# Softmax of a fused attention and MLP kernel: the scale moves into q on GpSimd, the row's small sums move between engines

## The chip, the cores and the metric

The kernel runs on one core of a Trainium2 chip. The core has five instruction queues that matter here, each worked off in order: TensorE (PE, with its weight loads PEld), VectorE (DVE), ScalarE (ACT), GpSimd (POOL) and SyncE (SP), from which all the DMAs are issued. The time is the device time of one execution in microseconds (us). The profile is that of one execution.

## What is computed

Eight batches of eight heads of attention over 576 positions with head width 64, and an MLP on the joined heads. Cut to what matters:

```python
scale = 1.0 / np.sqrt(q.shape[-1])                      # 1/8
scores = scale * np.matmul(q, k.transpose(0, 1, 3, 2))
thresh = np.max(scores, axis=-1, keepdims=True) - tau   # tau = 0.02
scores = np.where(scores >= thresh, scores, -1e9)
scores = scores - np.max(scores, axis=-1, keepdims=True)
attn = np.exp(scores)
attn = attn / (np.sum(attn, axis=-1, keepdims=True) + 1e-09)
out = np.matmul(attn, v)
# then, on out as (4608, 512):
h = x @ w_in                                            # 512 -> 2048
g = h * np.tanh(np.log1p(np.exp(np.minimum(h, 20.0))))  # for h <= 20
return g @ w_out                                        # 2048 -> 512
```

If tau is negative no score reaches its threshold; then all of a row's scores are -1e9, and the reference's row is uniform, 1/576.

## The kernel before, in words

Two heads make a pair; there are 32 pairs, and each has nine tiles of 128 rows of scores (2 x 576 rows), so the attention is a loop over 288 tiles, here numbered from 0. One tile goes through these steps, spread over several turns of the loop `for g in range(NT + 5)` (L665):

- PE multiplies 128 rows of q with 576 columns of k into the PSUM tile `s` (`scores`; two buffers).
- DVE takes the negated row maximum into column 0 of a small tile `st` (`row_max`), makes the scaled maximum (column 2) and the threshold (column 1, L405 and L406), and ACT makes `e = exp(scale * s + bias)` (L407).
- DVE multiplies `e` with the mask `s >= threshold` into `p` and sums the row into column 3 (`masked`, L412).
- In the next turn the sum's two small followers are made: column 5, 1/576 where the sum is 0 (`un`), and column 4, the sum plus 1e-9 (`de`), in `total` on DVE. From tile 54 on (`UNV`) column 5 is made by POOL in `masked` instead. Then `normalise`: DVE's RECIPROCAL makes column 6 from column 4, and POOL makes `p = p * reciprocal + un`.
- Two turns on, PE transposes `p`, ACT and DVE take it out of PSUM (`hi`, `lo`, `tk`), PE multiplies it with v (`y`), ACT copies y (`x`, `yo`) and POOL adds the two (`x<-x,yo`).

In the first four pairs (tiles 0 to 35) some operands are plain fp32: half of q (`a in plain`) and of k and all of v come by DMA straight into their tiles, and the rest, as all of q, k and v from tile 36 on, is split into a rounded part and a remainder. For q: the DMA brings a raw tile `r`, ACT casts all 128 rows to `q`, and POOL overwrites the lower 64 rows with the remainder `r - q` (L340 and L341). q is split in four pieces a pair, k in four, v in two. The raw tiles have four buffers.

Nothing here is put in order by a scheduler: `InOrder` (L82) chains each engine's instructions in the order in which the Python code makes them, so every engine's queue is the loop body as written. Only the DMAs on SP are moved by the framework. In a turn g, POOL's queue holds: `normalise` of tile g-1, the y adds, the splits of q, k, v and x that fall due ("chores"), parts of the w_in decoding (up to tile 53 or so), and, from tile 54 on, `un` of tile g. DVE's holds: maximum of g, `total` of g-1, threshold of g, RECIPROCAL of g-1, `lo` and `tk`, mask of g.

From tile 42 on, PE also runs the first MLP product, a number of matmuls a turn that a table (`MIX`) sets, so that it fills each turn; its results leave by ACT (`hst`). The table has 18 entries: the loop repeats itself every two pairs. After the attention come the last MLP pieces and the second product, which the change doesn't touch.

All of these instructions are issued by one helper line, so the profile shows L92 for each of them (L91 in the changed kernel): they are told apart by engine, operation and tile names. `st` is the small tile, `p<-p,st` on POOL is `normalise`, `p<-s,st,e` on DVE the mask.

Of the kernel before, what the change touches and what calls it, by code (L numbers as in the profile page):

```python
# [5 lines left out]
F32 = mybir.dt.float32  # L6
F32R = mybir.dt.float32r
U32 = mybir.dt.uint32
AF = mybir.ActivationFunctionType
ALU = mybir.AluOpType  # L10
# [4 lines left out]
P = 128  # L15
B, H, S, D = 8, 8, 576, 64
# [12 lines left out]
UNV = 54  # L29
# [6 lines left out]
HB = S // 2  # L36
# [36 lines left out]
SCALE = 1.0 / float(D) ** 0.5  # L73
# [4 lines left out]
def fv(ap):  # L78
    return ap.bitcast(F32)
# [78 lines left out]
def attention_moe(tc, q, k, v, tau, w_in, w_out, out):  # L158
    nc = tc.nc
    from contextlib import ExitStack  # L160

    with ExitStack() as outer:
# [8 lines left out]
        back = cst.tile([P, 1], F32, name="back")  # L171
# [95 lines left out]
        nc = Engines(tc)  # L267
        with ExitStack() as first:
# [6 lines left out]
            with ExitStack() as att:  # L275
# [36 lines left out]
                def prep(pi):  # L312
# [12 lines left out]
                    def part(src, n):  # L325
                        r = raw.tile([P, 320], F32, name="r")
                        nc.sync.dma_start(r[:, :n], src)
                        return r[:, :n]

                    def q_part(c):  # L330
                        a, half = divmod(c, 2)
                        sl = slice(half * 320, (half + 1) * 320)
                        at = slice(c * 320, (c + 1) * 320)
                        if a in plain:
                            nc.sync.dma_start(qs[a][:D, sl], q[pi, :D, at])
                            return skip
                        r = part(q[pi, :, at], 320)

                        def split():
                            nc.scalar.copy(qs[a][:, sl], r)  # L340
                            nc.gpsimd.tensor_tensor(qs[a][D:, sl], r[D:], fv(qs[a][D:, sl]), ALU.subtract)  # L341

                        return split
# [59 lines left out]
                def exponential(s, st, e):  # L403
                    nm = st[:, 0:1]
                    nc.vector.tensor_scalar(st[:, 2:3], nm, SCALE, None, ALU.mult)  # L405
                    nc.vector.tensor_scalar(st[:, 1:2], nm, -1.0, back, ALU.mult, ALU.subtract)  # L406
                    nc.scalar.activation(e, s[:, :, :HB], AF.Exp, bias=st[:, 2:3], scale=SCALE)  # L407

                def masked(g, s, st, e, p):
                    p = p.rearrange("p (a b) -> p a b", a=2)  # L410
                    th, su, un = (st[:, i:i + 1] for i in (1, 3, 5))
                    nc.vector.scalar_tensor_tensor(p, s[:, :, :HB], th, e, ALU.is_ge, ALU.mult, accum_out=su)  # L412
                    if g >= UNV:
                        nc.gpsimd.tensor_scalar(un, su, 0.0, 1.0 / S, ALU.is_le, ALU.mult)
                    return p

                def total(g, st):
                    if g < UNV:
                        nc.vector.tensor_scalar(st[:, 5:6], st[:, 3:4], 0.0, 1.0 / S, ALU.is_le, ALU.mult)
                    nc.vector.tensor_scalar(st[:, 4:5], st[:, 3:4], 1e-9, None, ALU.add)  # L420

                def normalise(st, p):
                    de, un, rc = (st[:, i:i + 1] for i in range(4, 7))
                    nc.vector.reciprocal(rc, de)
                    nc.gpsimd.tensor_scalar(p, p, rc, un, ALU.mult, ALU.add)
# [182 lines left out]
                NT = NPAIRS * 9  # L608
# [48 lines left out]
                pairs[0]["ops"], todo = prep(0)  # L657
                splits = [todo[i]() for i in FIRST[:3]]
                nc.sync.dma_start(back, tau)
# [3 lines left out]
                nc.vector.tensor_scalar(back, back, 1.0 / SCALE, None, ALU.mult)  # L663
                begin(0)
                for g in range(NT + 5):  # L665
# [28 lines left out]
                    if 1 <= g <= NT:  # L694
                        total(g - 1, tiles[g - 1]["st"])
# [255 lines left out]
```

## Time and profile before

| | |
|---|---|
| median of 3 runs | 1341.53 us (1339.64 to 1341.58) |
| the profiled execution | 1341.68 us, its span 1339.9 us |
| PE, DVE, ACT, POOL busy over the span | 98%, 84%, 74%, 65% |
| TensorE clock granted, mean | 0.995 |
| tiles 0 to 35 | first 117 us |
| tiles 36 to 53 | next 67 us |
| tiles 54 to 286 | 184 to 900.5 us |
| second product and the rest | last 439 us |

How to read it: the span is the time from the first to the last instruction on the core. The share of an engine that is busy is a mean over stages with different limits; a view by windows shows them apart. PE's matmuls overlap each other, and the ends of them are modelled, so that a PE that is shown busy need not be at its peak. In lists by time a row is: start, length, engine, line, operation, output and inputs, and in brackets how long the engine stood idle before it and what ended that. Instructions of one engine can overlap by some 0.05 to 0.1 us, so a row's length is a little more than the step to the next start.

### The profile page before, as it was taken

How to read it: one execution, taken by the hardware profiler on the slowest of the kernel's cores; microseconds unless marked ns; L12 is line 12 of the kernel's file. 1: busy time of each engine (PE TensorE's matmuls, PEld its weight loads, DVE VectorE, ACT ScalarE, POOL GpSimd, SP SyncE). 2: the span in 40 equal slices, each digit the busy share in tenths (PEclk: the TensorE clock that was granted, in tenths of full speed). 3: DMA queues.
4: the chain of work that ended last, by engine and by line, in shares of the span. 5: the costliest groups of instructions: out<-in, count | busy, mean ns of one | idle time of the engine just before them, and what ended most of it. 6: DMA issues, size and time to landing. Idle time of an engine off the chain costs nothing.

```text
span 1339.9 us, 29650 instructions
## 1 busy us (share of the span) xinstructions
PE 1317.0 (98%) x9799; PEld 1244.9 (93%) x9799; DVE 1123.4 (84%) x3018; ACT 989.0 (74%) x2052; POOL 872.7 (65%) x1191
## 2 busy tenths in 40 slices
PE   9998899999999999999999999999999999999998
PEld 7555889999999999999999999999979999999998
DVE  6999999999999999999999999995986666676664
ACT  5888788888888888888888888875665556555552
POOL 5778888788787887878878788763403333434431
PEclk9999999999999999999999999999999999999999
DMA  5333454333343333433334333314744443444440
GB/s 155 92 98 107 119 170 128 91 101 109 90 123 95 105 103 91 118 95 113 101 91 115 97 109 107 95 44 132 234 142 148 129 142 120 133 134 142 142 127 32
DMA packets 151913, 154.77 MB, mean 116 GB/s; under 512 B 35536, under 2 KB 128720, under 8 KB 151760
## 3 DMA queue, kind: packets, MB, share of 16 engines
q1 hardware_dynamic: 151760, 152.87, 38.3%
q8 instruction: 78, 1.28, 0.4%
q14 instruction: 75, 0.61, 0.1%
HBM read 105.64 MB, written 47.19 MB: 114 GB/s over the span
## 4 chain that ended last, share of the span: by engine, by line
PE 90%; DVE 5%; ACT 3%; issue 1%; DMA 1%; POOL 0%; DVEq 0%; ACTq 0%; POOLq 0%; SPq 0%
PE o L92 27%; PE h L92 27%; PE s L92 14%; PE y L92 12%; PE tp L92 9%; DVE st L92 1%; PE t L92 1%; DVE p L92 1%; DVE dec L92 1%; DVE w2l L92 1%; ACT e L92 1%; PE warm L92 1%; ACT w L92 0%; ACT dec L92 0%; DMA hd<-hst 0%
## 5 line engine op out<-in xcount | busy, mean ns | idle before, releaser
L92 PE MATMUL h<-xh,w1h 128*128 128x288 f32 x1024 | 302.3, 295 | 1.0 <-ACT hst L92 1.0
L92 PE MATMUL h<-xl,w1h 128*128 128x288 f32 x1024 | 302.4, 295 | 0.0
L92 PE MATMUL h<-xh,w1l 128*128 128x288 f32 x1024 | 302.2, 295 | 0.0
L92 POOL TENSOR_SCALAR p<-p,st 128x576 f32<-128x576 f32 x288 | 244.9, 850 | 57.7 <-DVE st L92 35.0
L92 POOL TENSOR_TENSOR z<-z 128x256 f32<-128x256 f32 x128 | 124.4, 976 | 223.0 <-DVE z L92 214.2
L92 PE MATMUL s<-k,q 128*128 128x288 f32 (+1 forms) x1280 | 253.5, 323 | 8.5 <-DVE p L92 8.2
L92 DVE SCALAR_TENSOR_TENSOR p<-s,st,e 128x576 f32<-128x576 f32 x288 | 235.1, 816 | 20.4 <-ACT e L92 10.4
L92 ACT ACTIVATE e<-s,st 128x576 f32<-128x576 f32 x288 | 214.4, 744 | 36.4 <-DVE st L92 31.7
L92 DVE TENSOR_TENSOR gl<-z,gh 128x1792 fp32r<-128x1792 f32 (+1 forms) x72 | 141.7, 1969 | 108.2 <-ACT gh L92 108.2
L92 ACT CAST gh<-z 128x1792 fp32r<-128x1792 f32 (+1 forms) x72 | 116.5, 1620 | 150.2 <-issue 81.2
L92 DVE TENSOR_REDUCE st<-s 128x1 f32<-128x576 f32 x288 | 216.7, 752 | 3.0 <-PE s L92 2.9
L92 PEld LDWEIGHTS s<-k,q 128*128 128x128 f32 (+1 forms) x1280 | 181.6, 189 | 38.3 <-DVE p L92 23.9
L92 DVE TENSOR_TENSOR lo<-tp,hi 128x512 fp32r<-128x512 f32 (+1 forms) x280 | 174.8, 633 | 49.6 <-ACT hi L92 42.7
L92 PEld LDWEIGHTS h<-xh,w1h 128*128 128x128 f32 x1024 | 192.5, 188 | 1.5 <-ACT hst L92 1.4
L92 PEld LDWEIGHTS h<-xh,w1l 128*128 128x128 f32 x1024 | 192.5, 188 | 0.0
L92 PEld LDWEIGHTS h<-xl,w1h 128*128 128x128 f32 x1024 | 192.4, 188 | 0.0
L92 PE MATMUL tp<-ident,p 128*128 128x128 f32 x1152 | 174.4, 274 | 3.6 <-DVE lo L92 2.4
L92 ACT CAST hi<-tp 128x512 fp32r<-128x512 f32 (+1 forms) x280 | 149.9, 546 | 35.8 <-PE tp L92 32.9
L92 PEld LDWEIGHTS tp<-ident,p 128*128 128x128 f32 x1152 | 138.9, 140 | 13.6 <-issue 5.7
L92 POOL TENSOR_TENSOR x<-x,yo 64x256 f32<-64x256 f32 (+1 forms) x112 | 89.9, 803 | 88.2 <-ACT yo L92 85.1
L92 PE MATMUL o<-gh,sl 128*128 128x256 f32 x512 | 144.5, 282 | 0.0
L92 PE MATMUL o<-gl,sh 128*128 128x256 f32 x512 | 143.8, 281 | 0.0
(76 smaller groups left out, 3249.8 us busy)
## 6 DMA issues: line engine op xcount, KB each, us to landing
z<-hd SPq DMA_DIRECT2D x144, 256.0 KB, 3.1
r<-q SPq DMA_DIRECT2D x120, 160.0 KB, 2.3
r<-k SPq DMA_DIRECT2D x120, 160.0 KB, 2.2
out_t<-c SPq DMA_DIRECT2D x36, 256.0 KB, 2.5
r<-v SPq DMA_DIRECT2D x56, 160.0 KB, 2.3
dec<-w_in SPq DMA_DIRECT2D x32, 256.0 KB, 3.1
hd<-hst SPq DMA_DIRECT2D x16, 512.0 KB, 3.3
w<-w_out SPq DMA_DIRECT2D x16, 512.0 KB, 4.5
```

The lines of the kernel that those rows point to most:

```text
L92: made = method(*args, **kwargs)
```

## The change

- q's pieces are multiplied by `slope` (the scale, 1/8, or 0 where tau is negative) on POOL, in place in the raw tile, before ACT casts them. The two plain pieces of each of the first four pairs, which came by DMA straight into place, now come into a raw tile too and go through POOL.
- `s` is then scaled already, so ACT's exponent takes the negated maximum (column 0) itself as its bias. The DVE instruction that scaled it (column 2) is gone from all 288 tiles.
- `un` is gone. With slope 0 all scores are 0; with the threshold raised to 3e38 below the maximum (`far`), all pass, and the row is uniform.
- `de`, the sum plus 1e-9, moves from DVE to POOL for all tiles, into `masked`. RECIPROCAL stays on DVE.
- tau is loaded first; three small DVE instructions make `slope`, `far` and `back` ahead of the first split.

```diff
-UNV = 54
...
-        back = cst.tile([P, 1], F32, name="back")
+        back, slope, far = (cst.tile([P, 1], F32, name=n) for n in ("back", "slope", "far"))
...
-                    def part(src, n):
+                    def part(src, n, rows=slice(0, P)):
                         r = raw.tile([P, 320], F32, name="r")
-                        nc.sync.dma_start(r[:, :n], src)
-                        return r[:, :n]
+                        nc.sync.dma_start(r[rows, :n], src)
+                        return r[rows, :n]
...
-                        if a in plain:
-                            nc.sync.dma_start(qs[a][:D, sl], q[pi, :D, at])
-                            return skip
-                        r = part(q[pi, :, at], 320)
+                        rows = slice(0, D) if a in plain else slice(0, P)
+                        r = part(q[pi, rows, at], 320, rows)
 
                         def split():
-                            nc.scalar.copy(qs[a][:, sl], r)
-                            nc.gpsimd.tensor_tensor(qs[a][D:, sl], r[D:], fv(qs[a][D:, sl]), ALU.subtract)
+                            if a in plain:
+                                nc.gpsimd.tensor_scalar(qs[a][:D, sl], r, slope[:D], 0.0, ALU.mult, ALU.add)
+                            else:
+                                nc.gpsimd.tensor_scalar(r, r, slope, 0.0, ALU.mult, ALU.add)
+                                nc.scalar.copy(qs[a][:, sl], r)
+                                nc.gpsimd.tensor_tensor(qs[a][D:, sl], r[D:], fv(qs[a][D:, sl]), ALU.subtract)
...
                     nm = st[:, 0:1]
-                    nc.vector.tensor_scalar(st[:, 2:3], nm, SCALE, None, ALU.mult)
                     nc.vector.tensor_scalar(st[:, 1:2], nm, -1.0, back, ALU.mult, ALU.subtract)
-                    nc.scalar.activation(e, s[:, :, :HB], AF.Exp, bias=st[:, 2:3], scale=SCALE)
+                    nc.scalar.activation(e, s[:, :, :HB], AF.Exp, bias=nm)
 
                 def masked(g, s, st, e, p):
                     p = p.rearrange("p (a b) -> p a b", a=2)
-                    th, su, un = (st[:, i:i + 1] for i in (1, 3, 5))
+                    th, su, de = (st[:, i:i + 1] for i in (1, 3, 4))
                     nc.vector.scalar_tensor_tensor(p, s[:, :, :HB], th, e, ALU.is_ge, ALU.mult, accum_out=su)
-                    if g >= UNV:
-                        nc.gpsimd.tensor_scalar(un, su, 0.0, 1.0 / S, ALU.is_le, ALU.mult)
+                    nc.gpsimd.tensor_scalar(de, su, 1e-9, None, ALU.add)
                     return p
 
-                def total(g, st):
-                    if g < UNV:
-                        nc.vector.tensor_scalar(st[:, 5:6], st[:, 3:4], 0.0, 1.0 / S, ALU.is_le, ALU.mult)
-                    nc.vector.tensor_scalar(st[:, 4:5], st[:, 3:4], 1e-9, None, ALU.add)
-
                 def normalise(st, p):
-                    de, un, rc = (st[:, i:i + 1] for i in range(4, 7))
-                    nc.vector.reciprocal(rc, de)
-                    nc.gpsimd.tensor_scalar(p, p, rc, un, ALU.mult, ALU.add)
+                    rc = st[:, 5:6]
+                    nc.vector.reciprocal(rc, st[:, 4:5])
+                    nc.gpsimd.tensor_scalar(p, p, rc, 0.0, ALU.mult, ALU.add)
...
                 pairs[0]["ops"], todo = prep(0)
+                nc.sync.dma_start(back, tau)
+                nc.vector.tensor_scalar(slope, back, 0.0, SCALE, ALU.is_ge, ALU.mult)
+                nc.vector.tensor_scalar(far, back, 0.0, 3e38, ALU.is_lt, ALU.mult)
+                nc.vector.tensor_tensor(back, back, far, ALU.add)
                 splits = [todo[i]() for i in FIRST[:3]]
-                nc.sync.dma_start(back, tau)
...
-                nc.vector.tensor_scalar(back, back, 1.0 / SCALE, None, ALU.mult)
...
-                    if 1 <= g <= NT:
-                        total(g - 1, tiles[g - 1]["st"])
```

How the queues move, at tiles 91 to 93, in the stretch where the loop has become regular. What a row waits for stands in brackets; of a semaphore's name the part ahead of the underscore is the engine that raises it, or a DMA's.

POOL before, from `un` of tile 91 to `normalise` of tile 92 (`st<-st` is `un`, `p<-p,st` is `normalise`, `q_4470<-r` a piece of q):

```order
L92 TENSOR_SCALAR st<-st 128x1 [waits DVE_49]
L92 TENSOR_SCALAR p<-p,st 128x576 [waits DVE_49,Pool_49]
L92 TENSOR_TENSOR x<-x,yo 64x320 [waits Activation_49,Pool_49]
L92 TENSOR_TENSOR q_4470<-r,q_4470 64x320 [waits DMAHW3_49,Activation_49]
L92 TENSOR_SCALAR st<-st 128x1 [waits DVE_49,Pool_49]
L92 TENSOR_SCALAR p<-p,st 128x576 [waits DVE_49,PE_49,Pool_49]
```

and after, the same stretch (`st<-st` is now `de`, `r<-r,slope` the scaling of q's piece):

```order
L91 TENSOR_SCALAR st<-st 128x1 [waits DVE_49]
L91 TENSOR_SCALAR p<-p,st 128x576 [waits DVE_49]
L91 TENSOR_TENSOR x<-x,yo 64x320 [waits Activation_49,Pool_49]
L91 TENSOR_SCALAR r<-r,slope 128x320 [waits DMAHW3_49,Pool_49]
L91 TENSOR_TENSOR q_4349<-r,q_4349 64x320 [waits Activation_49]
L91 TENSOR_SCALAR st<-st 128x1 [waits DVE_49,Pool_49]
L91 TENSOR_SCALAR p<-p,st 128x576 [waits DVE_49,PE_49]
```

The small instruction stays at its place in POOL's queue, behind the tile's adds and splits, but makes another number; one instruction is added ahead of the remainder of q.

DVE before, from RECIPROCAL of tile 91 to that of tile 92 (`st<-st 128x1 x2` are `de` of the tile before and the scaled maximum, `st<-st,back` is the threshold):

```order
L92 RECIPROCAL st<-st 128x1 [waits DVE_49]
L92 TENSOR_TENSOR lo<-tp,hi 128x4x128 [waits Activation_49]
L92 TENSOR_TENSOR tk<-t_4751,tk 64x128 [waits PE_49,Activation_49]
L92 TENSOR_TENSOR tk<-t_4751,tk 64x128
L92 SCALAR_TENSOR_TENSOR p,st<-s,st,e 128x576 [waits DVE_49,Activation_49]
L92 TENSOR_REDUCE st<-s 128x1 [waits PE_49,Pool_49]
L92 TENSOR_SCALAR st<-st 128x1 [waits DVE_49] x2
L92 TENSOR_SCALAR st<-st,back 128x1
L92 RECIPROCAL st<-st 128x1 [waits DVE_49]
```

and after:

```order
L91 RECIPROCAL st<-st 128x1 [waits Pool_49]
L91 TENSOR_TENSOR lo<-tp,hi 128x4x128 [waits Activation_49]
L91 TENSOR_TENSOR tk<-t_4623,tk 64x128 [waits PE_49,Activation_49]
L91 TENSOR_TENSOR tk<-t_4623,tk 64x128
L91 SCALAR_TENSOR_TENSOR p,st<-s,st,e 128x576 [waits DVE_49,Activation_49]
L91 TENSOR_REDUCE st<-s 128x1 [waits PE_49]
L91 TENSOR_SCALAR st<-st,back 128x1 [waits DVE_49]
L91 RECIPROCAL st<-st 128x1 [waits Pool_49]
```

Two small instructions are gone here (three in tiles 0 to 53), and RECIPROCAL waits for POOL, where it waited for DVE itself.

ACT before, at the next piece of q (`x<-y` and `yo<-y` are the copies of y):

```order
L92 COPY x<-y 64x256 [waits PE_49]
L92 COPY yo<-y 64x256 [waits Pool_49]
L92 CAST q_4470<-r 128x320 [waits DMAHW4_49]
L92 CAST k_4468<-r 128x320 [waits DMAHW5_49]
L92 CAST hi<-tp 128x4x128 [waits PE_49]
L92 ACTIVATE e<-s,st 128x576 [waits DVE_49,Activation_49]
```

and after:

```order
L91 COPY x<-y 64x256 [waits PE_49]
L91 COPY yo<-y 64x256 [waits Activation_49]
L91 CAST q_4349<-r 128x320 [waits Pool_49]
L91 CAST k_4347<-r 128x320 [waits DMAHW5_49]
L91 CAST hi<-tp 128x4x128 [waits PE_49]
L91 ACTIVATE e<-s,st 128x576 [waits DVE_49,Activation_49]
```

The order is the same; the cast of q waits for POOL's scaling instead of a DMA.

## The prediction

> **What bounds the kernel now.** I read the page's totals, then the windows by stage, then the groups of POOL and DVE, then the list by time at one tile. The page's first part:
>
> ```profile
> PE 1317.0 (98%) x9799; PEld 1244.9 (93%) x9799; DVE 1123.4 (84%) x3018; ACT 989.0 (74%) x2052; POOL 872.7 (65%) x1191
> ```
>
> PE is nearly always busy, which hides where the slack lies. By stage (columns: PE, PEld, DVE, ACT, POOL busy, clock, DMA):
>
> ```profile
> 0.00:117.00 117.00, 113.51 (x562) 69.92 (x563) 98.72 (x361) 87.11 (x220) 83.83 (x104) 1.00 0.40 118
> 117.00:184.00 67.00, 57.16 (x366) 48.40 (x365) 64.64 (x211) 54.39 (x140) 57.50 (x70) 0.95 0.45 133
> 184.00:900.50 716.50, 716.41 (x5501) 706.95 (x5500) 660.29 (x2152) 610.42 (x1468) 577.74 (x874) 1.00 0.36 102
> ```
>
> and the mask's instructions on DVE in the same windows (two rows a tile, so 36, 18 and 233 tiles):
>
> ```profile
> 0.00:117.00 117.00, 29.50 (x72) 1.00 0.40 118
> 117.00:184.00 67.00, 14.73 (x36) 0.95 0.45 133
> 184.00:900.50 716.50, 192.26 (x466) 1.00 0.36 102
> ```
>
> So from 184 us on a tile takes 716.5 / 233 = 3.075 us, 55.35 us for the 18 tiles after which the loop repeats; PE has no idle time there, DVE is busy 92%, POOL 81%. The first maximum stands at 7.33:
>
> ```profile
> 7.33 0.76 DVE L92 TENSOR_REDUCE st<-s 128x1 f32<-128x576 f32 x1 [2.75 <-PE s L92]
> ```
>
> The first 36 tiles thus take (117 - 7.3) / 36 = 3.05 us each, the next 18 take 3.72; there DVE (84% and 96%) is closest to the limit. What the change saves on DVE can shorten only these 54 tiles. What it does to POOL concerns all 288.
>
> **DVE, what is removed.** The list by time, DVE at tiles 91 and 92:
>
> ```profile
> 301.34 0.15 DVE L92 RECIPROCAL st<-st 128x1 f32<-128x1 f32 x1
> 302.23 0.59 DVE L92 TENSOR_TENSOR tk<-t,tk 64x128 fp32r<-64x128 f32 x2
> 302.86 0.82 DVE L92 SCALAR_TENSOR_TENSOR p<-s,st,e 128x576 f32<-128x576 f32 x1
> 303.60 0.75 DVE L92 TENSOR_REDUCE st<-s 128x1 f32<-128x576 f32 x1
> 304.27 0.27 DVE L92 TENSOR_SCALAR st<-st 128x1 f32<-128x1 f32 x2
> 304.58 0.15 DVE L92 RECIPROCAL st<-st 128x1 f32<-128x1 f32 x1
> 306.15 0.75 DVE L92 TENSOR_REDUCE st<-s 128x1 f32<-128x576 f32 x1
> ```
>
> Its group, 630 rows over the kernel, says 147 ns each (and no idle time ahead of RECIPROCAL, the last column):
>
> ```profile
> L92 DVE TENSOR_SCALAR st<-st 128x1 f32<-128x1 f32 x630 | 78.2, 147 | 0.1
> L92 DVE RECIPROCAL st<-st 128x1 f32<-128x1 f32 x288 | 44.1, 153 | 0.0
> ```
>
> and ACT's exponent of tile 93 in the list by time:
>
> ```profile
> 304.63 0.74 ACT L92 ACTIVATE e<-s,st 128x576 f32<-128x576 f32 x1
> ```
>
> The small rows overlap: the pair at 304.27 is 0.27 long in all and runs partly in the tail of the maximum (303.60 + 0.75 = 304.35). ACT's exponent starts at 304.63, 0.09 behind the pair's end. Started by the maximum itself it could start at 304.44, 0.19 earlier. A tile without `tk`, 2.55 us from maximum to maximum here, could then take DVE 2.4; one with `tk` (0.59 more, part of it covered) some 2.9. If that were all, the first 54 tiles would gain at most 54 x 0.19 = 10 us, and the stage that PE fills nothing.
>
> **POOL, what is added.** The groups, all tiles together:
>
> ```profile
> L92 POOL TENSOR_SCALAR p<-p,st 128x576 f32<-128x576 f32 x288 | 244.9, 850 | 57.7 <-DVE st L92 35.0 <-DVE dec L92 2.6 <-DMA dec<-w_in 1.6
> L92 POOL TENSOR_TENSOR k<-r,k 128x320 fp32r<-128x320 f32 x120 | 104.8, 880 | 9.8 <-ACT k L92 5.9 <-DMA r<-q 0.7
> L92 POOL TENSOR_TENSOR q<-r,q 64x320 fp32r<-64x320 f32 x120 | 104.6, 881 | 11.4 <-DMA r<-k 2.3 <-DVE p L92 1.7 <-DVE dec L92 1.3
> L92 POOL TENSOR_TENSOR xl<-x,xh 128x288 fp32r<-128x288 f32 x64 | 51.9, 812 | 12.3 <-ACT xh L92 12.3
> L92 POOL TENSOR_SCALAR st<-st 128x1 f32<-128x1 f32 x234 | 51.4, 220 | 8.4 <-DVE p L92 2.5
> L92 POOL TENSOR_TENSOR vs<-r,vs 128x320 fp32r<-128x320 f32 x56 | 49.1, 877 | 1.2 <-ACT vs L92 0.7
> L92 POOL TENSOR_TENSOR x<-x,yo 64x320 f32<-64x320 f32 x56 | 49.0, 875 | 65.4 <-ACT yo L92 64.1 <-DVE st L92 1.2
> L92 POOL TENSOR_TENSOR x<-x,yo 64x256 f32<-64x256 f32 x56 | 40.9, 731 | 22.8 <-ACT yo L92 21.0
> ```
>
> `de` costs POOL 0.22; from tile 54 on it replaces `un` at the same price. The scaling of a q piece is a TENSOR_SCALAR of 128x320. No row shows one; the nearest is `normalise` (850 ns for 576 elements) with the 128x1 row as its fixed part: 0.22 + 0.63 x 320/576 = 0.57. I take 0.55; the bounds are 0.47 (850 x 320/576) and 0.88 (the two-operand rows of 320). The Trainium skill (GPSIMD Engine Reference, 3.1 Elementwise and 4.1 Engine selection) has one-input work on GpSimd at about line rate, 1.03 cycles an element, but sends elementwise work to VectorE; at the 1.2 GHz of its example 320 elements would take an estimated 0.27 us and the sum below would be 27 us smaller. `normalise` at 850/576 = 1.48 ns an element disagrees, and I go by it.
>
> **The new wait, where I see the cost.** RECIPROCAL now waits for POOL's `de`, and behind it in DVE's queue stand `lo`, `tk` and the next mask. POOL at the same tiles:
>
> ```profile
> 301.26 0.22 POOL L92 TENSOR_SCALAR st<-st 128x1 f32<-128x1 f32 x1
> 301.67 0.83 POOL L92 TENSOR_SCALAR p<-p,st 128x576 f32<-128x576 f32 x1 [0.19 <-DVE st L92]
> 303.86 0.88 POOL L92 TENSOR_TENSOR x<-x,yo 64x320 f32<-64x320 f32 x1 [1.36 <-ACT yo L92]
> 304.70 0.89 POOL L92 TENSOR_TENSOR q<-r,q 64x320 fp32r<-64x320 f32 x1
> 305.68 0.22 POOL L92 TENSOR_SCALAR st<-st 128x1 f32<-128x1 f32 x1
> ```
>
> The row at 305.68 is the place where `de` of tile 92 will stand. The mask ended at 303.68, RECIPROCAL ran at 304.58: POOL comes there 2.0 us after the mask and 1.1 us after RECIPROCAL. Today nobody but POOL needs that row. After the change DVE stands still until it is done, and POOL in turn stands still until RECIPROCAL answers, since only `normalise` follows. From one RECIPROCAL to the next a tile then takes the longer of two loops: DVE's 2.4 or 2.9, and POOL's. The answers between engines, by rows:
>
> ```profile
> 941.43 2.45 POOL L92 TENSOR_TENSOR s<-s,w 128x1024 uint32<-128x1024 uint32 x1 [2.67 <-DVE s L92]
> 943.92 1.05 ACT L92 CAST w2h<-s 128x1024 fp32r<-128x1024 f32 x1 [1.69 <-POOL s L92]
> 13.42 0.15 DVE L92 RECIPROCAL st<-st 128x1 f32<-128x1 f32 x1
> 13.68 0.83 POOL L92 TENSOR_SCALAR p<-p,st 128x576 f32<-128x576 f32 x1 [1.64 <-DVE st L92]
> 2.96 0.46 ACT L92 CAST q<-r 128x320 fp32r<-128x320 f32 x1 [0.94 <-DMA r<-q]
> 3.56 0.86 POOL L92 TENSOR_TENSOR q<-r,q 64x320 fp32r<-64x320 f32 x1 [2.26 <-DMA r<-k]
> ```
>
> From POOL to ACT 0.04 (taken for POOL to DVE too; the other bound is the 0.19 above), from DVE to POOL 0.11, from ACT to POOL 0.14. POOL's loop without any split: `de` 0.22 + 0.04 + RECIPROCAL 0.15 + 0.11 + `normalise` 0.81 = 1.33 (of each POOL row I count 0.04 less than its length, for the overlap with the next). A piece of q grows from 0.84 to scaling 0.55 + 0.04 + cast 0.46 + 0.14 + 0.84 = 2.03, since scaling and remainder are neighbours in POOL's queue and the cast lies between them.
>
> For 18 tiles: 18 x 1.33 + 8 q x 2.03 + 8 k x 0.84 + 4 v x 0.84 + 4 x 0.83 and 4 x 0.69 for y + 4 xl x 0.77 = 59.4 us, already over 55.35. The loops are uneven: by the order in the queue they are, in us, 6.2, 1.3, 4.2, 1.3, 4.9, 2.9, 2.9, 3.8, 2.2, 4.2, 5.4, 3.0, 5.0, 2.0, 2.9, 2.0, 2.9, 2.2. Seven lie under DVE's loop, and filling them up adds 3.9: 63.3. Then the y adds wait for ACT, as they do now:
>
> ```profile
> POOL x L92 <- ACT yo L92: 85.1, 70, 7.7
> ```
>
> 85.1 us over 112 adds is 0.76 each; I charge it to the four adds that stand in a long loop behind a short one, where POOL is not late already: 3.0, in all 66.4 a cycle, 11.0 more than now.
>
> **The sum**, against the profiled execution's 1341.7 us (span 1339.9 and 1.8 around it; 0.15 above the median of the runs): 12 cycles from tile 54 to 269 give 12 x 11.0 = 132. The last 18 tiles have no loads left: +2. Tiles 0 to 35, with two split and two plain q pieces a pair and the w_in work on POOL, come by the same rule to 3.33 instead of 3.05 a tile, +10; tiles 36 to 53 to 4.3 instead of 3.7, +9. At the start tau is issued first, ahead of q,
>
> ```profile
> 2.12 0.43 SPq L659 DMA_DIRECT2D back<-tau  x1
> ```
>
> and the first scaling stands ahead of the first scores, 0.43 + 0.55: +1. The three small DVE instructions there run while DVE has nothing to do. Together +154: **1496 us**. Costed at nothing: ACT's cast waits for POOL with `hi`, the next exponent and `hst` behind it; it is covered because DVE waits too. Without that cover PE falls late, and the short loops cannot be shorter than PE's present tiles (3.24 and 2.55 above), some 19 us more. The eight plain q transfers now hold raw buffers; a raw buffer is freed later by what the loop is longer, and SP's queue with it, which I leave uncosted.
>
> **Bounds.** Scaling at 0.47 or 0.88: -8 or +32. The reply from POOL at 0.19 instead of 0.04: +21. No y waits: -36.
>
> **The rivals.** (A) The above: 1496. (B) Long and short loops even out, since ring buffers let DVE and POOL drift: then only POOL's total counts, 59.4 a cycle, +49 and some +8 before tile 54: 1399. For it: `s` and `p` have two buffers each. Against: RECIPROCAL and `de` tie the two engines in every tile, and no buffer lies between them. (C) PE, now with idle time in each long loop, gets a lower clock. The second window shows it, 0.95 over 67 us with PE busy 57 of 67, which is 6.7 us at half speed, 3.35 us of work lost. If each of the five longest loops of a cycle brought one such spell, 16.8 us of PE work would be lost against 11.0 of slack, 5.8 a cycle, 70 in all: 1566. For it: loops of 5 to 6 us with 3 us of PE work. Against: the first window kept 1.00. The Trainium skill (TensorE: Matmul & The Clock Gate, Part 1) has the clock halved after an idle window of about 3.4 us, which the uneven loops come close to. (D) Not slower: POOL is late in the trace only because nobody hurries it. If `de` ends within 0.9 us of the mask's end (303.68 to 304.58), RECIPROCAL waits for nothing, the 0.19 a tile is won in the first 54 tiles, and the time is 1331. It decides where POOL has no y add or split between `normalise` and `de`; in 16 of 18 tiles it has one. (E) The waits are real, but PE's work hides them and the gain pays for the rest: within 0.2%, about what a measurement of this kernel can tell from no change (its runs spread 0.15%): 1342.
>
> **How the numbers follow.** A 0.65, B 0.14, C 0.16, D 0.03, E 0.02. Slower 0.95, same 0.02, faster 0.03. The range takes in A with its bounds (1452 to 1549), goes down part of the way to B and up past C: 1430 to 1580; what it leaves out is most of B, D and E, under 2 in 10.
>
> **What would show it.** In the changed profile: DVE's idle time ahead of RECIPROCAL, ended by POOL's `st`, of the order of 100 us or more, where it was 0.0; the tiles of the regular stretch at some 3.7 us instead of 3.075 and uneven; PE idle there. POOL's scaling near 0.55 us with ACT's cast between it and the remainder. If RECIPROCAL hardly waits, the whole account is wrong; if it waits and tiles are near 3.3, B was right; a clock under 0.97 in the regular stretch means C.

## The result: 1616.7 us, slower by a fifth

The changed kernel takes 1616.66 us (median of 4 runs, 1611.8 to 1622.13), the kernel before 1341.36 beside it: a ratio of 1.206 (95% interval 1.202 to 1.210). The forecast, 1496 us with a range of 1430 to 1580, had the direction and named both new waits, one of them at no cost; it was 121 us short. The profiled execution of the changed kernel ran 1615.56 us, its span 1613.8, its mean granted clock 0.95.

The totals of the page, and the waits of the changed kernel (columns: who waited for whom, us in total, times, longest):

```profile
PE 1418.9 (88%) x9799; PEld 1309.7 (81%) x9799; DVE 1079.7 (67%) x2390; ACT 991.5 (61%) x2052; POOL 929.2 (58%) x1373
```

```profile
DVE st L91 <- POOL st L91: 350.8, 192, 4.9
...
ACT q L91 <- POOL r L91: 170.5, 120, 2.7
POOL x L91 <- ACT yo L91: 130.6, 98, 7.6
PEld tp L91 <- POOL st L91: 124.2, 66, 3.5
...
PE tp L91 <- DVE lo L91: 110.1, 64, 3.3
```

No engine is full any more; everyone waits for someone. The groups of instructions of the changed kernel (behind the bar: busy time, mean ns of one; then the idle time ahead of them and what ended it):

```profile
L91 DVE RECIPROCAL st<-st 128x1 f32<-128x1 f32 x288 | 46.3, 161 | 352.0 <-POOL st L91 350.8
L91 POOL TENSOR_SCALAR r<-r,slope 128x320 f32<-128x320 f32 x120 | 65.0, 541 | 8.1 <-DMA r<-q 2.7
L91 ACT CAST q<-r 128x320 fp32r<-128x320 f32 x120 | 55.1, 459 | 170.5 <-POOL r L91 170.5
L91 POOL TENSOR_TENSOR x<-x,yo 64x320 f32<-64x320 f32 x56 | 48.3, 862 | 93.3 <-ACT yo L91 93.3
L91 PE MATMUL tp<-ident,p 128*128 128x128 f32 x1152 | 184.3, 284 | 120.5 <-DVE lo L91 110.1 <-POOL dec L91 6.8 <-ACT pf L91 2.8
```

In the kernel before, the cast, PE's transposes and `lo` had these rows:

```profile
L92 ACT CAST q<-r 128x320 fp32r<-128x320 f32 x120 | 51.9, 456 | 2.4 <-DMA r<-q 1.6
L92 PE MATMUL tp<-ident,p 128*128 128x128 f32 x1152 | 174.4, 274 | 3.6 <-DVE lo L92 2.4 <-POOL dec L92 0.9 <-ACT pf L92 0.3
L92 DVE TENSOR_TENSOR lo<-tp,hi 128x512 fp32r<-128x512 f32 x224 | 153.7, 686 | 40.1 <-ACT hi L92 34.7
```

RECIPROCAL's idle time went from 0.0 to 352 us. One scaling takes 541 ns. New against the forecast are two things: ACT's cast, forecast as hidden, waits 1.4 us in each of 120 pieces, and PE's transposes wait 110 us for `lo`, where they waited 2.4.

How that looks in one tile: the list by time of the changed kernel, POOL, then ACT, DVE and PE (start, length, engine, operation, idle time before it and what ended that):

```profile
372.12 0.86 POOL L91 TENSOR_TENSOR x<-x,yo 64x320 f32<-64x320 f32 x1 [1.55 <-ACT yo L91]
372.96 0.53 POOL L91 TENSOR_SCALAR r<-r,slope 128x320 f32<-128x320 f32 x1
374.06 0.88 POOL L91 TENSOR_TENSOR q<-r,q 64x320 fp32r<-64x320 f32 x1 [0.57 <-ACT q L91]
375.04 0.53 POOL L91 TENSOR_SCALAR r<-r,slope 128x320 f32<-128x320 f32 x1
376.15 0.86 POOL L91 TENSOR_TENSOR q<-r,q 64x320 fp32r<-64x320 f32 x1 [0.57 <-ACT q L91]
377.10 0.21 POOL L91 TENSOR_SCALAR st<-st 128x1 f32<-128x1 f32 x1
...
371.62 0.42 ACT L91 COPY yo<-y 64x320 f32<-64x320 f32 x1
373.52 0.46 ACT L91 CAST q<-r 128x320 fp32r<-128x320 f32 x1 [1.49 <-POOL r L91]
375.61 0.46 ACT L91 CAST q<-r 128x320 fp32r<-128x320 f32 x1 [1.62 <-POOL r L91]
...
376.38 0.59 ACT L91 CAST hi<-tp 128x512 fp32r<-128x512 f32 x1
...
377.34 0.16 DVE L91 RECIPROCAL st<-st 128x1 f32<-128x1 f32 x1 [4.42 <-POOL st L91]
377.42 0.67 DVE L91 TENSOR_TENSOR lo<-tp,hi 128x512 fp32r<-128x512 f32 x1
...
378.24 0.63 PE L91 MATMUL tp<-ident,p 128*128 128x128 f32 x4 [3.11 <-DVE lo L91]
```

Read it as one chain. ACT copies `yo`, POOL adds it, and only then scales the piece of q that stands behind the add; ACT's next instruction, the cast, waits for that, and POOL's remainder waits for the cast. A second piece repeats it. `de` follows at 377.10; RECIPROCAL has stood since 372.9, `lo` behind it, PE's transposes behind `lo`. PE then delivers the next y late, so ACT's copies and POOL's next add come late.

The stages, from the starts of DVE's row maxima in the list by time (us; "a cycle" is the mean of the twelve cycles of 18 tiles from tile 54 to 269):

| kernel | start | tiles 0 to 35 | 36 to 53 | a cycle | 270 to 286 | the rest | span |
|---|---|---|---|---|---|---|---|
| before | 7.3 | 108.6 | 67.8 | 55.3 | 52.3 | 439.9 | 1339.9 |
| changed | 8.7 | 128.4 | 81.5 | 73.7 | 65.4 | 445.6 | 1613.8 |
| `de` on DVE, q scaled | 8.1 | 127.1 | 77.4 | 65.9 | 59.2 | 444.5 | 1506.6 |
| `de` on POOL, q not scaled | 7.4 | 117.3 | 76.3 | 63.2 | 58.5 | 439.9 | 1457.7 |

### The profile page after: what moved, and what is told of

It is laid out like the page before. It is cut to its first block, busy times and chain, and to the rows that moved or that the text cites. A ratio compares the mean times of both kernels' runs of the same rounds, so it can differ in the third digit from the quotient of the medians.

```text
span 1613.8 us, 28802 instructions
## 1 busy us (share of the span) xinstructions
PE 1418.9 (88%) x9799; PEld 1309.7 (81%) x9799; DVE 1079.7 (67%) x2390; ACT 991.5 (61%) x2052; POOL 929.2 (58%) x1373
## 3 DMA queue, kind: packets, MB, share of 16 engines
q8 instruction: 78, 1.28, 0.3%
## 4 chain that ended last, share of the span: by engine, by line
PE 39%; POOL 26%; DVE 15%; issue 9%; ACT 8%; DMA 1%; POOLq 0%; SPq 0%; DVEq 0%; ACTq 0%
PE o L91 23%; PE y L91 7%; POOL q L91 5%; POOL k L91 4%; POOL p L91 4%; DVE st L91 4%; PE h L91 4%; POOL r L91 4%; DVE lo L91 4%; DVE p L91 4%; POOL x L91 3%; PE s L91 3%; PE tp L91 2%; POOL st L91 2%; ACT x L91 2%
## 5 line engine op out<-in xcount | busy, mean ns | idle before, releaser
L91 PE MATMUL h<-xh,w1h 128*128 128x288 f32 x1024 | 309.8, 303 | 1.0 <-ACT hst L91 0.9
L91 PE MATMUL h<-xl,w1h 128*128 128x288 f32 x1024 | 309.9, 303 | 0.0
L91 PE MATMUL s<-k,q 128*128 128x288 f32 (+1 forms) x1280 | 265.4, 334 | 48.3 <-DVE p L91 45.0
L91 PE MATMUL tp<-ident,p 128*128 128x128 f32 x1152 | 184.3, 284 | 120.5 <-DVE lo L91 110.1
L91 POOL TENSOR_SCALAR p<-p,st 128x576 f32<-128x576 f32 x288 | 220.7, 766 | 117.1 <-DVE st L91 115.2
L91 DVE RECIPROCAL st<-st 128x1 f32<-128x1 f32 x288 | 46.3, 161 | 352.0 <-POOL st L91 350.8
L91 PEld LDWEIGHTS s<-k,q 128*128 128x128 f32 (+1 forms) x1280 | 189.6, 196 | 91.8 <-DVE p L91 71.6
L91 PEld LDWEIGHTS h<-xh,w1h 128*128 128x128 f32 x1024 | 199.1, 194 | 3.0 <-ACT hst L91 1.9
L91 PEld LDWEIGHTS h<-xl,w1h 128*128 128x128 f32 x1024 | 200.4, 196 | 0.0
L91 POOL TENSOR_TENSOR x<-x,yo 64x256 f32<-64x256 f32 (+1 forms) x112 | 89.3, 798 | 131.7 <-ACT yo L91 130.6
L91 ACT CAST q<-r 128x320 fp32r<-128x320 f32 x120 | 55.1, 459 | 170.5 <-POOL r L91 170.5
```

What stands on the lines that cost most here:

```text
L91: made = method(*args, **kwargs)
```

## The experiments

Ratios are to the kernel before, timed beside them, with the 95% interval. The changed kernel's two parts were first taken apart.

**1. `de` back on DVE; q still scaled on POOL.**

```diff
-                    nc.gpsimd.tensor_scalar(de, su, 1e-9, None, ALU.add)      # in masked
+                    nc.vector.tensor_scalar(st[:, 4:5], st[:, 3:4], 1e-9, None, ALU.add)   # in total, as before
```

> The changed kernel with the sum's 1e-9 (de) back on VectorE, ahead of RECIPROCAL; the scaling of q on GpSimd and the rest of the change stay. Theory (the tie): the time was lost because RECIPROCAL waits in every tile for GpSimd to reach de behind its adds and splits. Without that wait a tile of the regular stretch is back at TensorE's 3.08 us, 55.4 us for 18 tiles, and the first 54 tiles gain up to 0.19 us each: 1331 to 1345 us. Rival (the q path): scaling, cast and remainder of q as a chain over GpSimd, ScalarE and GpSimd is what costs, 1.1 us for each of 8 pieces in 18 tiles (measured from scaling to remainder in the changed kernel), with ScalarE's queue held up behind it: 8.8 us more for 18 tiles, about 1341 + 115 = 1455 us.

1509.3 us, 1.125 (1.123 to 1.126). The theory fell: with the tie between DVE and POOL gone, 168 us are left. The rival's sum, 1455, was too small as well. Of what is left, 126 us lie in the cycles, 18.5 in tiles 0 to 35 and 4.6 in "the rest". Groups of this kernel:

```profile
L91 DVE RECIPROCAL st<-st 128x1 f32<-128x1 f32 x288 | 44.0, 153 | 0.0
L91 ACT CAST q<-r 128x320 fp32r<-128x320 f32 x120 | 55.1, 459 | 162.2 <-POOL r L91 162.2
L91 DVE TENSOR_TENSOR lo<-tp,hi 128x512 fp32r<-128x512 f32 x224 | 153.9, 687 | 201.8 <-ACT hi L91 200.5
```

RECIPROCAL waits for nothing, but the cast still waits 162 us, and `hi` stands behind the cast, `lo` behind `hi`. One place in its list by time, POOL and then ACT:

```profile
422.60 0.88 POOL L91 TENSOR_TENSOR x<-x,yo 64x320 f32<-64x320 f32 x1 [1.39 <-ACT yo L91]
423.57 0.54 POOL L91 TENSOR_SCALAR r<-r,slope 128x320 f32<-128x320 f32 x1
...
422.04 0.42 ACT L91 COPY yo<-y 64x320 f32<-64x320 f32 x1
424.14 0.46 ACT L91 CAST q<-r 128x320 fp32r<-128x320 f32 x1 [1.69 <-POOL r L91]
```

ACT waits 1.69 us for work that POOL could begin only after ACT's own `yo`: the add's 0.88 and the scaling's 0.54 and the steps between. POOL's queue order made the cast depend on the copy just ahead of it.

**2. `de` on POOL; q not scaled, the scale in the exponent and in DVE's scaled maximum as before.** `un` stays out, so the uniform row of a negative tau is left out.

```diff
-                                nc.gpsimd.tensor_scalar(r, r, slope, 0.0, ALU.mult, ALU.add)
...
+                    nc.vector.tensor_scalar(st[:, 2:3], nm, SCALE, None, ALU.mult)
-                    nc.scalar.activation(e, s[:, :, :HB], AF.Exp, bias=nm)
+                    nc.scalar.activation(e, s[:, :, :HB], AF.Exp, bias=st[:, 2:3], scale=SCALE)
```

> The changed kernel with q's scaling taken out (q loaded and split as before, the scale in ScalarE's exponent, the scaled maximum on VectorE again); de stays on GpSimd, and the empty-row flag stays out. Theory (the tie): 8 pieces of q cost 1.1 us less each, so 71.9 - 8.8 = 63.1 us for 18 tiles instead of 55.4, 8 us over for 12 such cycles, and some 20 us in the first 54 tiles: 1430 to 1470 us. Rival (the q path): nothing is left that costs, 1335 to 1350 us.

1459.4 us, 1.088 (1.086 to 1.089). So the tie alone costs 118 us, q's path alone 168, both 275. The expectation of the tie theory for this kernel held, but it is not the whole. In the mean of the regular cycles the two add, 7.9 + 10.5 = 18.4 us with 18.4 measured; in tiles 0 to 35 they do not (8.7 and 18.5 alone, 19.8 together). The clock has a part in these figures (rival C below). In the cycles in which experiment 1 has the full clock it takes 65.1, so that the sum is 17.7, against 16.6 more than before in the changed kernel's shortest cycles, at 0.98: the sum holds to about 1 us a cycle.

**3. POOL's y adds one turn later, all else as changed.**

```diff
-                        nc.gpsimd.tensor_tensor(xs, xs, yo[mn, :n], ALU.add)
+                        later.append(lambda: nc.gpsimd.tensor_tensor(xs, xs, yo[mn, :n], ALU.add))
...
+                    while later:
+                        later.pop(0)()
```

> The changed kernel with GpSimd's add of the two halves of y issued one turn of the loop later, ahead of that turn's splits; nothing else moves. In the changed kernel GpSimd stood idle ahead of these adds for 7.3 us in 18 tiles. If these waits belong to GpSimd's loop, as the sum of the prediction had it (there with 3.0 us), 18 tiles fall from 71.9 us towards 65 to 67 and the kernel to 1540 to 1570 us. If they only fill time in which another wait would stand, it stays at 1600 to 1620 us.

1541.8 us, 1.149 (1.147 to 1.151), as expected: 75 us less. The y adds hardly wait now (13.2 us in all, where it was 131.7), and the cast's wait for POOL fell from 170.5 to 113.5.

**4. Neither wait: ACT scales while it casts, POOL scales only the half that it needs, behind the cast; no `de`.** RECIPROCAL takes the row sum itself, which is never 0, since the maximum adds exp(0).

```diff
-                                nc.gpsimd.tensor_scalar(r, r, slope, 0.0, ALU.mult, ALU.add)
-                                nc.scalar.copy(qs[a][:, sl], r)
+                                nc.scalar.activation(qs[a][:, sl], r, AF.Copy, scale=slope)
+                                nc.gpsimd.tensor_scalar(r[D:], r[D:], slope[D:], 0.0, ALU.mult, ALU.add)
...
-                    nc.vector.reciprocal(rc, st[:, 4:5])
+                    nc.vector.reciprocal(rc, st[:, 3:4])
```

> The change without its two costs: de is left out (RECIPROCAL takes the row's sum itself, which is at least 1 since the row's maximum has exponent 0 and passes the mask, so that adding 1e-9 does not change it in fp32), and q is scaled by ScalarE in its cast, while GpSimd scales the lower 64 rows behind the cast and then takes the remainder, so that ScalarE waits for no one new. VectorE has one small instruction fewer than the changed kernel with de on VectorE. Theory (the tie): TensorE's 55.4 us for 18 tiles in the regular stretch, and 0.06 to 0.19 us less for each of the first 54 tiles: 1329 to 1340 us, faster than before by up to 1%. Rival (the q path): GpSimd still has one instruction more for each piece; 1341 us or up to 10 us more.

1354.2 us, 1.0087 (1.0073 to 1.0101), just above the rival's range and far above the other's. POOL scales as many pieces as in the changed kernel (in the same 0.54 us each, with the one 128x1 instruction a tile gone), and the cycle is 55.5 us. The groups of the cast, now an ACTIVATE, and of the scaling:

```profile
L91 ACT ACTIVATE q<-r,slope 128x320 fp32r<-128x320 f32 x120 | 64.0, 557 | 0.8
L91 POOL TENSOR_SCALAR r<-r,slope 64x320 f32<-64x320 f32 x120 | 65.1, 542 | 20.8 <-POOL p L91 4.6 <-ACT q L91 4.4 <-issue 1.4
```

The cast waits for nobody. In all, POOL is busy 872.0 us here, no longer than before (872.7), since `un` is gone and `normalise` is shorter. That the scaling as work costs little is seen against the second kernel of experiment 10, which has neither the scaling nor `de`: POOL busy 800.7, a cycle of 55.3. So 71 us more of work on POOL cost next to nothing in the cycles; the order of the hand-overs costs it. Of the 12.5 us by which this kernel's span is longer than before, 2.4 are at the start, where ACT's ACT_TABLE_LOAD, 1.28 us long, stands behind a transfer of q (at 3.68 us instead of 0.73), and 5.8 in "the rest", where nothing was changed (experiment 9).

**5. Experiment 1 with the scaling moved ahead of the y add.** In the turn in which a piece is split, POOL scales it right behind `normalise`.

```diff
                         normalise(tiles[g - 1]["st"], tiles[g - 1]["p"])
+                    for work in chores.get(g, []):
+                        getattr(work, "scaled", skip)()
```

> The first experiment (`de` on DVE, q scaled on POOL: 1509.3) with one thing moved: POOL scales a piece of q in the same turn, but right behind `normalise`, ahead of the y add, and no longer right ahead of the cast. The same instructions, on the same engines. Theory: what costs is that ACT's cast stands behind POOL's scaling, the scaling behind POOL's y add, and the y add behind ACT's own copy `yo`, so that ACT waits about 1.5 us in each piece and DVE's `lo` with it. Then the waits of ACT's cast go from 162 us to under 40, and the time to 1350 to 1390. Rival: the extra work on POOL, or a hand-over from POOL to ACT as such, costs it; then the time stays above 1450.

1371.8 us, 1.025 (1.020 to 1.029). The same instructions on the same engines; POOL's order alone takes away 137 of the 168 us. The groups:

```profile
L91 ACT CAST q<-r 128x320 fp32r<-128x320 f32 x120 | 53.9, 459 | 43.8 <-POOL r L91 42.4
L91 DVE TENSOR_TENSOR lo<-tp,hi 128x512 fp32r<-128x512 f32 x224 | 154.3, 689 | 76.7 <-ACT hi L91 70.8
```

The cast's 42 us are a little over the "under 40" expected; `lo` waits 125 us less. A cycle takes 56.9.

**6. The changed kernel with the same move.**

> The changed kernel, with the same move: scaling right behind `normalise`. Theory (the two new waits are separate and add up: 118 us for `de` alone, 168 for q alone, 275 for both): what is left is the wait for `de`, so 1455 to 1500. Rival (they share one loop, and taking the one away leaves the other at its full size in the loop): above 1540.

1487.0 us, 1.109 (1.107 to 1.111), as the theory had it: 130 us less. The tie's 118 and the 30 that experiment 5 has left make 148; 145 are left here. Each of the two waits can be taken away without the other.

**7. Both moves: scaling ahead, and y adds a turn later.**

> The changed kernel with both moves: scaling right behind `normalise` (alone: 1487.0) and POOL's y adds one turn later (alone: 1541.8, so 75 us less than the changed kernel). Theory: the wait for `de` itself is mostly POOL standing behind y adds that wait for ACT; with those a turn later POOL reaches `de` earlier, and 40 to 75 us of what is left go: 1410 to 1450. Rival: the y adds only cost through the scaling that stood behind them; with the scaling moved they are worth little more: above 1470.

1479.3 us, 1.104 (1.102 to 1.107): the theory missed. Groups of experiment 6 (first two rows) and of this one:

```profile
L91 POOL TENSOR_TENSOR x<-x,yo 64x320 f32<-64x320 f32 x56 | 48.7, 870 | 41.8 <-ACT yo L91 41.7
L91 POOL TENSOR_TENSOR q<-r,q 64x320 fp32r<-64x320 f32 x120 | 103.8, 874 | 16.2 <-ACT q L91 12.0
```

```profile
L91 POOL TENSOR_TENSOR x<-x,yo 64x320 f32<-64x320 f32 x56 | 48.6, 867 | 11.0 <-ACT yo L91 8.7
L91 POOL TENSOR_TENSOR q<-r,q 64x320 fp32r<-64x320 f32 x120 | 103.8, 875 | 57.8 <-ACT q L91 56.1
```

The add no longer waits for ACT's `yo`, and the remainder behind it waits for ACT's cast instead: the wait moved within POOL's queue, and `de` comes as late as before: RECIPROCAL waits 223.5 us instead of 225.8, and a cycle takes 64.0 instead of 64.1. The 75 us of experiment 3 came from the scaling that stood behind the adds.

**8. What the tie costs by: RECIPROCAL behind `lo` and `tk`.** Experiment 2 with only that move on DVE (so it too leaves out the uniform row), and its control, the kernel before with the move.

```diff
-                        normalise(tiles[g - 1]["st"], tiles[g - 1]["p"])
                     if 3 <= g < NT + 3:
                         if not full:
                             lo_main(*old)
...
+                        normalise(tiles[g - 1]["st"], tiles[g - 1]["p"])
```

> The experiment with `de` on POOL and q unscaled (1459.4), with one thing moved: in each turn RECIPROCAL comes behind `lo` and `tk` in DVE's queue instead of ahead of them; POOL's queue is the same. From tile 36 on. Theory: the wait for `de` costs because `lo` stands behind it, and PE's transposes and ACT behind `lo`; then most of the 118 us go: 1350 to 1410. Rival: the closed loop costs it (RECIPROCAL, `normalise`, y adds and splits on POOL, `de`, and the next RECIPROCAL, with the mask of the tile between), whatever else is queued; then the time stays at 1440 to 1470.

> The control: the kernel before, `de` on DVE, with the same move of RECIPROCAL behind `lo` and `tk`. It tells what the move itself costs, since `normalise` on POOL and the transposes of p then come later by the 0.7 to 1.3 us of `lo` and `tk`: 1341 to 1360 by both theories, nearer 1341 if POOL has that time to spare.

1413.2 us, 1.054 (1.052 to 1.055), and 1356.6, 1.011 (1.010 to 1.013). The first lies just above the theory's range. Against the control the tie costs 57 us instead of 118. Groups of experiment 2, then of this one:

```profile
L91 DVE RECIPROCAL st<-st 128x1 f32<-128x1 f32 x288 | 46.4, 161 | 181.6 <-POOL st L91 179.8
L91 PE MATMUL tp<-ident,p 128*128 128x128 f32 x1152 | 178.4, 278 | 44.0 <-DVE lo L91 38.0 <-POOL dec L91 5.1 <-ACT pf L91 0.2
```

```profile
L91 DVE RECIPROCAL st<-st 128x1 f32<-128x1 f32 x288 | 46.8, 163 | 99.1 <-POOL st L91 94.9
L91 PE MATMUL tp<-ident,p 128*128 128x128 f32 x1152 | 175.3, 275 | 3.2 <-DVE lo L91 1.8 <-POOL dec L91 0.7 <-ACT pf L91 0.6
```

PE's wait for `lo` is gone. About half of the tie was what stood behind RECIPROCAL. The cycle is still 60.2 us against the control's 56.6; that this other half is the loop of `normalise`, splits, `de` and RECIPROCAL itself is what remains, and no experiment of its own shows it.

**9. The 5.7 us in "the rest".** The second product is not touched, yet PE, busy throughout, gets through fewer matmuls in the changed kernel (669 from 1400 to 1480 us). The kernel before with two more constant tiles, never used:

```diff
-        back = cst.tile([P, 1], F32, name="back")
+        back, slope, far = (cst.tile([P, 1], F32, name=n) for n in ("back", "slope", "far"))
```

> The kernel before, with two more 128x1 constant tiles set aside beside `back` and never used; no instruction differs. In the second product (the last 440 us) the changed kernel starts a matmul every 120.0 ns and the kernel before every 118.0 ns on average, though PE is busy all the time at full clock in both; so do the three experiments that hold `slope` and `far` (120.0) and the one that does not (118.0). Theory: it is the place of the later tiles in memory, which the two constants shift. Then the step is 120.0 ns here too and the time is 1345 to 1348 us. Rival: it comes with the scaling of q, or with the order of the transfers at the start. Then the step stays at 118.0 and the time at 1340 to 1343.

1345.4 us, 1.0028 (1.0019 to 1.0037). One window of the second product (PE, PEld, DVE, ACT, POOL busy with their instructions, clock), the kernel before first, then this one:

```profile
1140.00:1220.00 80.00, 80.00 (x680) 80.00 (x680) 54.01 (x48) 43.15 (x34) 31.68 (x32) 1.00 0.43 135
```

```profile
1140.00:1220.00 80.00, 80.00 (x669) 80.00 (x668) 52.16 (x46) 43.17 (x34) 31.58 (x32) 1.00 0.40 130
```

680 matmuls in 80 us against 669, without one instruction changed. The two constants are taken to shift the later tiles on their side of memory by 64 bytes, 32 each; the traces hold no addresses. Other shifts:

> The kernel before with one unused constant more, which shifts the later tiles on that side by 32 bytes (two gave 64 bytes, a matmul step of 120.0 ns in the second product and 1345.4 us). If any shift costs it, the step is 120.0 ns and the time 1344 to 1347; if it goes by the position within 64 or 128 bytes, it may be 118.0 or less, and the time at or below 1342.

> The kernel before with three unused constants more, a shift of 96 bytes. As for the shift of 32: 120.0 ns and 1344 to 1347 if any shift costs it; 118.0 ns or less and 1342 or less if it goes by position within 64 or 128 bytes and this is a good one.

One constant more gives 1343.0 us, 1.0008 (0.9999 to 1.0016), between its two ranges, with 679 matmuls in the same window; three more give 1340.6, 0.9994 (0.9985 to 1.0002), with 680. So not every shift costs it, and none of those tried beats the kernel before.

**10. The savings alone.** The kernel before without `un` and `de`, once with `slope` as the exponent's scale and once with the constant (the latter leaves out the uniform row):

```diff
-                    nc.vector.reciprocal(rc, de)
-                    nc.gpsimd.tensor_scalar(p, p, rc, un, ALU.mult, ALU.add)
+                    nc.vector.reciprocal(rc, st[:, 3:4])
+                    nc.gpsimd.tensor_scalar(p, p, rc, 0.0, ALU.mult, ALU.add)
```

> The kernel before without `un` and without `de` (the row that holds the maximum adds exp(0) = 1, so the sum is never 0), RECIPROCAL on the row sum itself; q is not scaled, ACT's exponent takes `slope` as its scale from a register of the constants, DVE scales the maximum with it, and the three constants share one tile so that nothing is shifted. Theory (small DVE and POOL instructions cost only where they are waited for): the regular stretch stays at 55.4 us for 18 tiles, since PE fills it; the first 54 tiles lose one to two small DVE instructions of some 0.13 us each and gain 3 to 8 us: 1333 to 1339. Rival (those are hidden there too): 1340 to 1343.

> The kernel before without `un` and `de`, RECIPROCAL on the row sum, and nothing else: the exponent's scale is the constant 1/8 as before. It leaves out the uniform row of a negative tau. It bounds from above what the change's savings of small instructions can bring. Rival 1, they are worth something in the first 54 tiles, where PE is not full: 1333 to 1338. Theory, they lie beside other work there too: 1339 to 1343. The experiment with slope as the exponent's scale, 1344.6, differs from this one by ACT's exponent, 835 instead of 744 ns there, so it should come out 1 to 6 us above this one.

1344.6 us, 1.0023 (1.0014 to 1.0032), above both of its ranges, and 1341.1, 1.0001 (0.9992 to 1.0010), as its theory had it. The small instructions that could be saved are worth nothing: they lie beside other work. With `slope` the exponent is longer; its group in the kernel before and in the first of these:

```profile
L92 ACT ACTIVATE e<-s,st 128x576 f32<-128x576 f32 x288 | 214.4, 744 | 36.4 <-DVE st L92 31.7
```

```profile
L91 ACT ACTIVATE e<-s,st,back 128x576 f32<-128x576 f32 x288 | 240.6, 835 | 42.8 <-DVE st L91 36.2 <-DVE dec L91 0.5
```

A scale read from memory costs 91 ns an instruction. The Trainium skill (ScalarE: Activation LUTs, What ACT_TABLE_LOAD costs) gives about 93 ns for each such operand; the rows agree.

## Why the prediction was wrong, by its own steps

| term | forecast | measured |
|---|---|---|
| twelve cycles | 132 (11.0 each) | 220.3 (18.4 each) |
| tiles 0 to 35 | 10 | 19.8 |
| tiles 36 to 53 | 9 | 13.7 |
| last 18 tiles | 2 | 13.1 |
| start | 1 | 1.3 |
| second product and the rest | 0 | 5.7 |
| sum | 154 | 273.9 |

**The step that failed is the one costed at nothing:** "ACT's cast waits for POOL with `hi`, the next exponent and `hst` behind it; it is covered because DVE waits too". Experiment 1 takes DVE's wait away and 168 us remain; experiments 2 and 6 take the cast's wait away (2.1 and 57.5 us of its 170.5 are left) and 157 and 130 us go. It was not covered: the two waits follow one another through `hi`, `lo`, PE's transposes and y, and in the cycles they add. The 19 us that the forecast named for "without that cover" is far too small: experiment 1 alone loses 126 us in the cycles. The forecast saw only PE being late, not that POOL's y adds, ahead of the next scaling, would be later for it; this last is the reading of the rows above, which experiments 3, 5 and 7 support.

**The y adds, a term with a price of its own.** The forecast charged 3.0 us a cycle for them. In tiles 90 to 107 of the changed kernel they wait 7.2 us, but they wait 5.5 there in the kernel before, at no cost, and 7.0 in experiment 2, where no q is scaled. Experiment 7 takes nearly all of that wait away, and the cycle stays as it was. So their waiting is not a term to be added: it costs what stands behind them in POOL's queue, here the scaling.

**Rival C, the clock, was true in part.** Its sign was a clock under 0.97 in the regular stretch; the changed kernel has 0.94 there, the kernel before 1.00. The stretch, and four of its cycles (length; PE, PEld, DVE, ACT, POOL busy; clock):

```profile
218.60:1102.80 884.20, 742.66 (x5093) 702.62 (x5092) 584.62 (x1560) 570.03 (x1368) 576.64 (x915) 0.94 0.28 79
440.50:512.50 72.00, 59.65 (x427) 56.38 (x426) 48.61 (x131) 47.52 (x114) 48.15 (x77) 0.98 0.29 80
512.50:586.40 73.90, 61.32 (x427) 57.82 (x426) 48.70 (x131) 47.43 (x114) 47.94 (x77) 0.95 0.28 77
586.40:662.20 75.80, 64.60 (x427) 61.39 (x426) 48.82 (x131) 47.51 (x114) 47.92 (x77) 0.89 0.27 76
662.20:734.20 72.00, 59.62 (x427) 56.37 (x426) 48.68 (x131) 47.52 (x114) 47.93 (x77) 0.98 0.29 80
```

The same 427 matmuls, and the length goes with the clock: up to 3.9 us a cycle. Over the twelve, 884.2 - 12 x 71.9 = 21 us, where C had 70 on top of A. The clock is lower outside the cycles too: 0.87 in tiles 36 to 53 (0.95 before) and 0.95 in tiles 0 to 35 (1.00 before). In experiment 1 tiles 0 to 35 have 0.88; an estimate of what that takes from PE, (1 - 0.88) x 127.1 = 15 us, is most of the 18.5 us that they lose. That the clock alone makes these differences was read from the rows and not tried. The Trainium skill (TensorE: Matmul & The Clock Gate, Part 1) has the clock halved after about 3.4 us of idleness; PE's wait of 3.11 us above is of that order, and no run here tells where the limit lies.

**What was right, and what else was not.** RECIPROCAL waits hundreds of us for POOL's `st`; a scaling takes 541 ns (0.55 taken); tiles are uneven, as in A and against B, which would have had 59.4 a cycle: 73.7 were measured, and 63.2 even without q's path. D and E were wrong, and the savings on DVE are worth nothing (experiment 10), also in the first 54 tiles, where the forecast had allowed at most 10 us. It had read DVE as closest to the limit there, but in the first window PE is busy 113.5 of 117 us and DVE 98.7. A small slip: by its own 4.3 against 3.72 us a tile, tiles 36 to 53 come to +10, not +9. The early tiles and the last 18 were charged by the same rule without ACT's waits, and came out short by 10, 5 and 11 us; q's path alone costs tiles 0 to 35 18.5 us (experiment 1, with the lower clock), and 2.5 with the scaling moved (experiment 5, clock 1.00). Of the rest's 5.7 us, 4.6 come without any new wait, with nothing but two unused constants added (experiment 9), which the forecast did not look at.

What stays open: why two more constants slow the second product, what lowers the clock, and how much of the tie's second half is which part of POOL's queue.

## What to carry to other kernels

When a step is put between two engines, write down for each of them what stands *ahead* of the new instruction in its queue and whom that waits for; here the cast on ACT came to depend, through POOL's queue, on ACT's own copy just before it, and moving the same instruction ahead of the y add in POOL's queue was worth 130 us. Two waits on different engines are not covered by one another because both engines stand still: follow what each holds back until they meet, and if they meet in one chain, add them; here that came out to about 1 us a cycle. And where an edit adds a constant or a small tile, compare the speed of stages that it does not touch before blaming the edit.

## What the runs showed of the hardware that was not expected

- A matmul of 256 columns in the second product starts every 118 ns on average in the kernel before (80 us / 680) and every 120 ns (80 / 669) when two unused constants are set aside (taken as 64 bytes), at a granted clock of 1.00 in both. The time between two starts varies around 118 ns in the first and is 120 in nearly every one of the second.
- `normalise` on POOL takes 766 ns (128 x 576) with a constant as its addend, where it took 850 with a column of `st`:

```profile
L91 POOL TENSOR_SCALAR p<-p,st 128x576 f32<-128x576 f32 x288 | 220.7, 766 | 117.1 <-DVE st L91 115.2 <-PE s L91 1.1 <-PE y L91 0.8
```

The scaling has the same form, a column and a constant, and takes 541 ns for 320 elements. From the two, an estimate: 0.88 ns an element and 0.26 us ahead of the first one. The prediction's 1.48 ns an element counted the fixed part, and the column as addend, as time per element.

- The granted clock can stay at half for 30 us with PE shown as busy throughout. From 19 to 49 us, experiment 1 and then the kernel before:

```profile
19.00:49.00 30.00, 30.00 (x84) 17.49 (x83) 14.52 (x45) 13.52 (x35) 12.22 (x17) 0.50 0.12 34
19.00:49.00 30.00, 30.00 (x149) 17.91 (x149) 24.47 (x77) 23.28 (x59) 22.64 (x32) 1.00 0.23 67
```

PE had waited 3.49 us just before, until 17.32. In experiment 5 it waits 3.62 us at the same place, and the clock is 1.00 from 19 to 49 us. So the length of the wait alone does not decide it.
